# Batch 0 of an FNet and gated-FFN kernel: even sequence rows regrouped by s mod 4 and summed as two 64-row tiles over half the columns

## The chip, the cores and the metric

The kernel runs on one core of one Trainium2 chip. The metric is the device time of one execution in microseconds (us). The engines are named as the profile names them: PE is TensorE (matmul; PEld is its weight load), DVE is VectorE, ACT is ScalarE, POOL is GpSimd, SP is SyncE, which issues nearly all transfers; SPq is its queue.

## What is computed

```python
batch, seq, dim = 8, 3008, 256                  # x: float32
X = np.fft.fft(x, axis=1); X = np.fft.fft(X, axis=2)
t = X.real.astype(np.float32).reshape(24064, 256)
gate = 1.0 / (1.0 + np.exp(-(t @ w_gate)))      # w_gate, w_val: 256 x 1536
out  = (gate * (t @ w_val)) @ w_out             # w_out: 1536 x 256
```

The three weights come as float64 and are brought to float32 on the chip, piece by piece.

## The kernel before

**Sequence transform.** With S = 3008 and M = S/2, the four rows s, S-s, M+s and M-s are folded into each other, so that a batch has 768 row slots (s from 0 to 752, the rest weighted zero). They lie as s = 6p + q: partition p of 128, slot q of 6. `half_rows` does this fold for batch 0 on DVE, in four steps over the slots `(0, 1)`, `(2, 3)`, `(4,)`, `(5,)` (`SLICES`). The folded rows are matmul weights (128 rows by 128 features); what streams past them are the tables `ST[0]` (cosine) and `ST[1]` (sine), each with 128 partitions, 6 slots and 753 columns: 377 even frequencies (`NE`), then 376 odd ones (`NO`). Because s = 6p + q, the parity of q is the parity of s. `half` keeps the sums over even slots in one PSUM bank (`ev`) and those over odd slots in another (`od`); `places` writes ev + od to frequency k and ev - od to M - k, for the cosine into the tile `pk`, for the sine into `qk`. `e_sums(1)` does the same for the one feature column that stands by itself: weights of one column, cosine table only, four column groups of PE (`at_`), result `er`, stored to DRAM as `ed`.

Later batches come in another way (`quarter`: four tiles of 32 rows); the change does not touch them.

**Weights.** `weight_load(j)` loads piece j (512 KB), `weight_parts(j)` takes its two halves apart on ACT, `weight_join(j)` puts them together with three DVE instructions and one POOL addition, and `weight_use(j)` calls `merge`, which multiplies the piece with the feature transform `dt` on PE and copies the two results out on ACT to `G2` and `G1`.

**Main loop.** Step i handles 128 of the 1536 hidden units for 252 frequencies: `front_a` (weights G1, streams `pk`) and `front_b` (weights G2, streams `qk`) fill the bank `pf`, `gate_a` and `gate_b` make the gated product, `back` multiplies with w_out. In the first steps the loop also merges the later weight pieces: piece 2 right after `front_b(0)`, pieces 3 and 5 around `front_b(1)`, and so on.

**Order.** The order of each engine is the order of the program text. The part before the loop is written out by hand: first all loads on SP, in the order in which they are to be used, then weight pieces 0 and 1, then four steps of fold and sums, then `places`. Every transfer from SP takes one of eight completion semaphores in turn, and waits for the transfer that had it before.

**Transfers of other shapes.** Two kinds of transfer later in this kernel matter for reading the change. `run` (L163) copies rows of the next batches from DRAM to DRAM with access patterns of 4 by 32 by 256 elements on both sides. `table_rows` (L206) copies rows of the tables to `rtab`, in DRAM too, with patterns of 2 by 32 by 753 on both sides. The loads at the start have 128 partitions as the outermost size of the side in SBUF, and 128 or 512 rows in DRAM.

```python
    def load_rows(q, n):
        nc.sync.dma_start(out=X[0][0:NP, :, q : q + n], in_=xf[0, :, :, q : q + n])
    def load_table(t, q, n, lo=0, hi=NE + NO):
        nc.sync.dma_start(out=ST[t][0:NP, q : q + n, lo:hi], in_=stab[:, t, q : q + n, lo:hi])
```

Of the kernel before, what the change touches and what calls it, by code (L numbers as in the profile page):

```python
# [8 lines left out]
F32 = mybir.dt.float32  # L9
# [3 lines left out]
ALU = mybir.AluOpType  # L13
# [68 lines left out]
def kernel(  # L82
# [52 lines left out]
    def bank(name, other=None):  # L135
        if other is not None:
            return pso.tile([P, 512], F32, name=name, tag=f"po{other}")
        return psx.tile([P, 512], F32, name=name, tag="x")
# [49 lines left out]
    table = const.tile([2, 1], F32, name="table")  # L188
    ed = dram.tile([B, NK + 1], F32, name="ed")

    def load_rows(q, n):
        nc.sync.dma_start(out=X[0][0:NP, :, q : q + n], in_=xf[0, :, :, q : q + n])  # L192

    def load_table(t, q, n, lo=0, hi=NE + NO):
        nc.sync.dma_start(out=ST[t][0:NP, q : q + n, lo:hi], in_=stab[:, t, q : q + n, lo:hi])

    NQ4 = NE // 4 + 1
    TILES = [(g, par, par * HP + g * TB) for g in range(2) for par in range(2)]
# [204 lines left out]
    def weight_use(j):  # L403
        w, c = jobs[j]
        if w == 2:
            WO[c] = WS.pop(j)
        else:
            merge(WS.pop(j), w, c, (4, 2, 3)[next(turns) % 3] if j > 1 else None)

    def merge(ws, g, c, other):  # L410
        cs = slice(c * WC, (c + 1) * WC)
        ps = bank("ps", other)
        for h in range(2):
            for t in range(2):
                mm(ps[:, h * WC : (h + 1) * WC], dt[:, t, h * HD : (h + 1) * HD], ws[:, t, :],
                   h == 0 and t == 0, t == 1)
        nc.scalar.copy(G2[:, g, cs], ps[:, WC : 2 * WC])
        nc.scalar.copy(G1[:, g, cs], ps[:, 0:WC])
        for f in range(c * WC // P, (c + 1) * WC // P):
            nc.sync.dma_start(  # L420
                out=ge[:, g, f : f + 1], in_=G2[0:1, g, f * P : (f + 1) * P])
# [60 lines left out]
    TURN = {}  # L482
    MORE = {}

    SLICES = ((0, 1), (2, 3), (4,), (5,))

    def fold_ops(b, nq):
        x4 = X.pop(b)
# [40 lines left out]
        if b:  # L529
            ops += [lambda q=q: feat(pool, *parts[1], q) for q in qs]  # L530
            for i, op in enumerate((ALU.add, ALU.subtract)):
                for ds in (slice(0, HD), slice(HD, D)):
                    ops.append(lambda i=i, op=op, ds=ds: pool.tensor_tensor(
                        x4[:, 3, i * N3 : (i + 1) * N3, ds], x4[:, 1, 0:N3, ds],
                        x4[:, 1, N3:, ds], op=op))
            parts[0] = x4[:, 3], x4[:, 1]
            slots = x4.rearrange("p i q d -> p (i q) d")
            tan = TAB["tan"], TAB["less"]

            def swap(blk):  # L540

                hs, here, there = (((1, 3), slice(0, HD), slice(HD, D)), ((0, 2), slice(HD, D), slice(0, HD)))[blk]
                for g, par, lo in TILES:
                    o = lo + (TB, -TB)[g]
                    for h in hs:
                        nc.sync.dma_start(out=x4[lo : lo + TB, h, :, there], in_=x4[o : o + TB, h, :, here])

            def more(v, blk, c, q):

                here, there = ((slice(0, HD), slice(HD, D)), (slice(HD, D), slice(0, HD)))[blk]  # L550
                here, there = (v[..., ds] for ds in (here, there))
                nc.vector.scalar_tensor_tensor(out=here, in0=there, scalar=c[:, q : q + 1], in1=here,
                                               op0=ALU.mult, op1=ALU.add)
            MORE[b] = ([lambda: swap(0), lambda: swap(1)],
                       [lambda q=q, a=a: more(slots[:, 9 + q : 19 + q : 9] if a == 0 else slots[:, (0, 21, 6)[a] + q],
                                              0, TAB[("other", "cx", "cy")[a]], q)
                        for q in range(N3) for a in range(3)],
                       [lambda q=q, a=a: more(slots[:, q + N3 : q + N3 + 10 : 9] if a else slots[:, q : q + 16 : 15],
                                              1, TAB["other"][:, N3:], q) for q in range(N3) for a in range(2)])

            def turn(q, minus):

                y = [slots[:, q : q + 16 : 15], slots[:, q + N3 : q + N3 + 10 : 9]]
                if minus:
                    y.reverse()
                nc.vector.scalar_tensor_tensor(
                    out=y[0][:, :, HD:D], in0=y[1][:, :, 0:HD], scalar=tan[minus][:, q : q + 1],
                    in1=y[0][:, :, 0:HD], op0=ALU.mult, op1=ALU.add)
            TURN[b] = [lambda q=q, minus=minus: turn(q, minus) for q in range(N3) for minus in range(2)]
            ops += [lambda q=q: feat(pool, *parts[0], q) for q in qs]  # L570
        else:

            def half_rows(q):
                even, odd = slice(0, 4, 2), slice(1, 4, 2)
                point(nc.vector, even, odd, q)
                first(nc.vector, even, odd, q)
                for blk in range(2):
                    across(nc.vector, blk, q)
                v, r = x4[:, 0:2, q], x4[:, 2:4, q]
                for to, op in ((r, ALU.subtract), (v, ALU.add)):  # L580
                    nc.vector.tensor_tensor(to[:, :, :, 1:HD], v[:, :, :, 1:HD], v[:, :, :, D - 1 : HD : -1],
                                            op=op)
                nc.vector.memset(r[:, :, :, 0:1], 0.0)
            ops += [lambda q=q: half_rows(slice(q[0], q[-1] + 1)) for q in SLICES]
        for blk, (v, r) in enumerate(parts):
            if b and blk:
                W[b, blk] = v[:, :, HD:D], r[:, :, HD:D]
# [4 lines left out]

    PQE = {}

    def half(b, w, d, blk, sn, other=None):


        c0, n = ((0, NE), (NE, NO))[blk]
        ev, od = [bank(name, other and other[i])[:, 0:n] for i, name in enumerate(("ev", "od"))]

        def sums(*qs):
            for q in sorted(qs, key=lambda q: q % 2):
                mm((ev, od)[q % 2], w(q), ST[int(sn)][0:NP, q, c0 : c0 + n], q < 2, q >= NQ - 2)

        def then():
            a = evp.tile([P, NE], F32, name="a", tag="a")[:, 0:n]
            nc.scalar.copy(a, ev)
            return lambda: places(d, blk, sn, a, od)
        return sums, then

    def places(d, blk, sn, ev, od, ends=(0, 1)):
        if 0 in ends:
# [64 lines left out]
        for t in PQE[b]:  # L677
            nc.vector.memset(t[:, NK:], 0.0)

    def seq_group(b, blk, what, other=None):  # L680
        return half(b, lambda q: W[b, blk][what][:, q, :], PQE[b][what], blk, what == 1, other)


    def e_load(b):
        nc.sync.dma_start(out=x8[:, b - 1], in_=xf[b, :, :, :, HD : HD + 1])

# [9 lines left out]
    def e_sums(m=B - 1):  # L696


        ps = bank("pe", NB - 1)
        at_ = lambda blk, par: slice((2 * blk + par) * TB, (2 * blk + par) * TB + m)  # L700

        def sums(*qs):
# [249 lines left out]
    nc.gpsimd.dma_start(out=zero, in_=nil)  # L952
    nc.scalar.dma_start(out=dt, in_=dtab.rearrange("(c p) d -> p c d", p=P))
    load_x(0)
    for j in range(2):
        weight_load(j)
    load_rows(0, 2)
    load_table(0, 0, 2)
    load_rows(2, 2)
    load_table(1, 0, 2, 0, NE)  # L960
    load_table(0, 2, 2)
    load_rows(4, 1)
    load_table(0, 4, 1)
    load_rows(5, 1)
    weight_load(2)
    load_table(1, 2, 2, 0, NE)
    load_table(0, 5, 1)
    load_table(1, 4, 2, 0, NE)
    load_table(1, 0, NQ, NE)
    for j in (3, 5, 6, 8, 9, 4, 7):  # L970
        weight_load(j)

    e0 = shared["qk"][:, 4 * WC : 4 * WC + CH]
    nc.gpsimd.memset(e0, 0.0)
    weight_parts(0)
    weight_parts(1)
    weight_join(0)
    weight_join(1)
    warm = bank("warm", 2)
    for i in range(4):  # L980
        mm(warm[:, 0:WC], dt[:, 0, 0:P], dt[:, 0], True, True)
    weight_use(0)
    weight_use(1)
    seq_start(0)

    cos = [seq_group(0, blk, 0, (2 * blk, 2 * blk + 1)) for blk in range(2)]
    e_, e_even = e_sums(1)
    sin = [seq_group(0, 0, 1)]
    for q, f in zip(SLICES, fold_ops(0, 2), strict=True):
        f()  # L990
        e_(*{1: (0, 1), 5: (2, 3, 4, 5)}.get(q[-1], ()))
        sin[0][0](*{5: (3,)}.get(q[-1], ()))
        cos[0][0](*q)
        cos[1][0](*q)
        sin[0][0](*{1: (0, 1), 4: (2,), 5: (4, 5)}.get(q[-1], ()))
    places_c = [cos[blk][1]() for blk in range(2)]
    weight_parts(2)
    weight_join(2)
    rest, *ends = e_even()
    rest()  # L1000
    for f in ends:
        f()
    for f in places_c:
        f()
    nc.scalar.copy(e0[0:1], E0[0][:, 0:CH])
    weight_parts(3)
    weight_join(3)
    sin.append(seq_group(0, 1, 1, (0, 1)))
    sin[1][0](*range(NQ))
    for j in range(KEEP, KEEP + 3):  # L1010
        weight_load(j)
    places_s = [group[1]() for group in sin]
    for f in places_s:
        f()
    e_rows(0)

    per = NFT * len(chunks)
# [2 lines left out]
    def at(i, *fs):  # L1020
        side.setdefault(i, []).extend(fs)
# [21 lines left out]
    for i, f in zip((1, 2, 2, 2, 3, 4, 4, 4, 5, 6, 6, 8, 8, 8, 9, 9, 9, 9, 10, 10, 10, 11, 11), quarter_x(1), strict=True):  # L1043
        at(i, f)
    at(i0 + 1, lambda: load_x(1))
    for b in range(1, B):
        at(20 + b, lambda b=b: e_load(b))
    at(3 * i0, e_fold)
# [197 lines left out]
```

## Time and profile before

| | |
|---|---|
| median of 3 runs | 1908.45 us (1908.44 to 1908.66) |
| profiled execution, its time | 1909.15 us |
| its span in the profile | 1907.4 us |
| PE busy | 1895.6 us (99%) |
| POOL, DVE, ACT busy | 1543.4, 1520.6, 1353.2 us |
| first `pf` matmul of the main loop | at 33.05 us |
| granted TensorE clock | 1.00 |

The span runs from the first to the last instruction of the program; 1.75 us of the execution lie around it. From the first `pf` matmul on, PE works through the rest of the program with almost no gap, so the stretch before it is looked at by itself: it holds the loads, the fold, and the sums of batch 0. A "pass" below is one matmul row of the profile; each float32 matmul of the program makes two.

### The profile page before, as it was taken

The numbers are of one execution on the slowest core, as the hardware profiler recorded it, in microseconds if no ns is written. First come the engines' busy times: TensorE is split into PE (matmuls) and PEld (weight loads), VectorE is DVE, ScalarE is ACT, GpSimd is POOL, SyncE is SP. The second block draws the span as 40 slices with busy tenths as digits, with TensorE's granted clock in tenths as the row PEclk, the third lists the DMA queues.
The fourth block names the chain that finished last, engine by engine and source line by source line (L and its number), as shares of the span: only waits on it lengthen the run. The fifth ranks groups of instructions, "written<-read, shape, count | busy, mean of one in ns | idle before, by whom it ended". The sixth has DMA issues, their size and how long they took to land.

```text
span 1907.4 us, 36057 instructions
## 1 busy us (share of the span) xinstructions
PE 1895.6 (99%) x11836; PEld 1756.6 (92%) x11836; DVE 1520.6 (80%) x3375; ACT 1353.2 (71%) x3235; POOL 1543.4 (81%) x2733
## 2 busy tenths in 40 slices
PE   8999999999999999999999999999999999999999
PEld 5788999999999999999999999999999999999998
DVE  7678888878979778897788878888788777977775
ACT  4777777777777777777777777677767777777775
POOL 2489879987999779997799878999789986877770
PEclk9999999999999999999999999999999999999999
DMA  8446221212022121211211212122120110010001
GB/s 315 120 134 80 71 89 51 72 33 81 21 64 54 31 87 32 62 41 37 89 39 48 45 39 81 40 52 58 30 74 17 36 37 15 15 25 17 15 18 30
DMA packets 197333, 109.33 MB, mean 57 GB/s; under 512 B 134823, under 2 KB 188818, under 8 KB 195354
## 3 DMA queue, kind: packets, MB, share of 16 engines
q1 hardware_dynamic: 196568, 106.50, 21.1%
q8 instruction: 95, 1.56, 0.3%
q14 instruction: 92, 0.75, 0.1%
q10 hardware_dynamic: 546, 0.51, 0.1%
q0 software_dynamic: 32, 0.00, 0.0%
HBM read 71.24 MB, written 47.87 MB: 62 GB/s over the span
## 4 chain that ended last, share of the span: by engine, by line
PE 94%; DMA 2%; SPq 1%; POOL 1%; ACT 1%; DVE 0%; issue 0%; ACTq 0%; POOLq 0%
PE pf L133 49%; PE po L133 41%; PE sum L133 2%; DMA rtab<-in_stab_dram 1%; PE ps L133 1%; POOL sf L824 1%; DMA st<-in_stab_dram 1%; SPq L206 1%; DMA raw<-in_moe_w_val_dram 0%; PE od L133 0%; POOL x L507 0%; SPq L192 0%; SPq L375 0%; PE pe L133 0%; PE ev L133 0%
## 5 line engine op out<-in xcount | busy, mean ns | idle before, releaser
L824 POOL TENSOR_TENSOR sf<-h,sf 128x168 f32<-128x168 f32 (+1 forms) x1104 | 621.0, 582 | 79.5 <-DVE h L818 75.9
L824 POOL TENSOR_TENSOR sf<-h 128x168 f32<-128x168 f32 (+1 forms) x920 | 519.3, 584 | 159.8 <-DVE h L818 158.0
L133 PE MATMUL pf<-qk,G 128*128 128x252 f32 (+1 forms) x2304 | 583.4, 376 | 0.9 <-ACT ae L787 0.8
L133 PE MATMUL pf<-pk,G 128*128 128x252 f32 (+1 forms) x2304 | 582.7, 376 | 0.0
L772 ACT ACTIVATE pf<-ek,ge 128x252 f32<-128x252 f32 (+1 forms) x1142 | 538.2, 471 | 23.2 <-DMA ge<-G 3.0
L133 PE MATMUL po<-sf,wf 128*128 128x168 f32 (+1 forms) x2944 | 508.3, 305 | 0.0
L787 ACT ACTIVATE ae<-pf 128x504 f32<-128x504 f32 (+1 forms) x576 | 338.8, 588 | 218.7 <-PE pf L133 217.2
L133 PEld LDWEIGHTS pf<-pk,G 128*128 128x128 f32 x2304 | 435.9, 190 | 53.3 <-ACT pf L772 1.5
L133 PE MATMUL po<-h,wf 128*128 128x168 f32 (+2 forms) x2584 | 461.3, 307 | 0.0
L133 PEld LDWEIGHTS po<-sf,wf 128*128 128x128 f32 x2944 | 453.4, 190 | 8.0
L818 DVE TENSOR_TENSOR h<-pf,z 128x252 f32<-128x252 f32 (+1 forms) x576 | 240.4, 417 | 274.0 <-ACT pf L815 270.5
L802 DVE TENSOR_TENSOR z<-ae,pf 128x504 f32<-128x504 f32 (+1 forms) x576 | 384.6, 668 | 83.1 <-ACT h L801 79.1
L908 DVE TENSOR_TENSOR c<-c 128x168 f32<-128x168 f32 (+1 forms) x920 | 438.7, 500 | 3.3
L133 PEld LDWEIGHTS pf<-qk,G 128*128 128x128 f32 x2304 | 410.6, 190 | 32.3 <-ACT ae L787 2.1
L133 PEld LDWEIGHTS po<-h,wf 128*128 128x128 f32 x2584 | 410.4, 190 | 17.8 <-issue 0.9
L801 ACT ACTIVATE h<-pf 128x252 f32<-128x252 f32 (+1 forms) x576 | 216.9, 376 | 146.3 <-PE pf L133 129.0
L815 ACT ACTIVATE pf<-z 128x252 f32<-128x252 f32 (+1 forms) x576 | 214.3, 372 | 116.4 <-DVE h L814 114.5
L814 DVE TENSOR_TENSOR h<-h,pf 128x252 f32<-128x252 f32 (+1 forms) x576 | 232.9, 404 | 0.0
L824 POOL TENSOR_TENSOR sf<-sf 128x168 f32<-128x168 f32 (+1 forms) x184 | 101.7, 553 | 14.4
L824 POOL TENSOR_TENSOR sf<-sf,h 128x168 f32<-128x168 f32 (+1 forms) x184 | 110.1, 598 | 0.0
L891 ACT COPY c<-po 128x504 f32<-128x504 f32 (+1 forms) x138 | 78.5, 569 | 0.0
L918 DVE STREAM_TRANSPOSE os<-c 128x256 f32<-128x256 f32 x188 | 76.5, 427 | 0.1
(158 smaller groups left out, 876.4 us busy)
## 6 DMA issues: line engine op xcount, KB each, us to landing
x<-xr SPq DMA_DIRECT2D x14, 1536.0 KB
out_dram<-os SPq DMA_DIRECT2D x376, 56.0 KB
xr<-in_xf_dram SPq DMA_DIRECT2D x105, 128.0 KB
x<-x SPq DMA_DIRECT2D x112, 96.0 KB
xr<-in_xf_dram SPq DMA_DIRECT2D x14, 384.0 KB
ek<-ed SPq DMA_DIRECT2D x40, 126.0 KB
out_dram<-os SPq DMA_DIRECT2D x288, 7.0 KB
xr<-in_xf_dram SPq DMA_DIRECT2D x21, 124.0 KB
```

What stands on the lines that cost most here:

```text
L133: nc.tensor.matmul(o, l, r, start=start, stop=stop, skip_group_check=True)
L772: nc.scalar.activation(PF[i][:, g], EK[i // NFT], AF.Copy, scale=ge[:, g, f : f + 1])
L787: nc.scalar.activation(AP[i], PF[i], AF.Copy, scale=2.0)
L801: nc.scalar.activation(H[p][:, fh, 0:n], PF[i][:, 0], AF.Sigmoid)
L802: nc.vector.tensor_tensor(z[:, :, ::-1], AP.pop(i), PF[i], op=ALU.subtract)
L814: nc.vector.tensor_tensor(h[:, fh, 0:n], h[:, fh, 0:n], pf[:, 1], op=ALU.mult)
L815: nc.scalar.activation(pf[:, 0], z[:, 0], AF.Sigmoid)
L818: nc.vector.tensor_tensor(h[:, fh, n:], pf[:, 0], z[:, 1], op=ALU.mult)
L824: nc.gpsimd.tensor_tensor(block(p, dst), block(p, a), block(p, b), op=(ALU.subtract, ALU.add)[op])
L891: (nc.vector.tensor_copy if t == 1 or t == 3 else nc.scalar.copy)(C[0][:, 3 * t * R : 3 * (t + 1) * R], PO[t][:, 0 : 3 * R])
L908: nc.vector.tensor_tensor(t[:, dst * R : (dst + 1) * R], *v, op=(ALU.subtract, ALU.add)[op])
L918: nc.vector.transpose(os_[0][0][:, s, 0:nb, h, :], t[:, c0 : c0 + nb * TB])
```

## The change

Slots 0, 2 and 4 (even s) are filled anew. `PAIR` names, for each of the three, one residue of s modulo 12 that goes to partitions 0 to 63 (s divisible by 4) and one that goes to partitions 64 to 127 (s = 2 modulo 4). `pair` makes the access pattern in DRAM: it takes two rows out of every pair of old partitions and puts the choice between the two outermost (size 2), then 64, then the row. `load_rows` uses it for an even slot, in four transfers (one for each of the four folded rows); `load_table` uses it for an even slot of a table.

`seq_sums` takes the place of `half`. For even slots it sums the two halves of the partitions separately (`x` and `y`, two banks), each as a 64-row tile, and only over the columns `H0` to `H1`, 377 of 753; `join` makes the other columns from sums and differences of x and y. Odd slots are as before: 128 rows, all columns. The order before the loop is new: the odd slots 1 and 3 are loaded, folded and summed first; weight piece 1 is loaded, joined and merged late; the outer columns of the cosine table's even slots, which only `e_sums` reads, come as six more transfers. `load_again` restores the cosine table's even slots to the old order in step 20 of the loop, for a later use. In `e_sums(1)` the order of slots becomes 1, 3, then 0, 2, 4, 5.

```diff
+    PAIR = {0: ((0, 0), (0, 2)), 2: ((0, 4), (1, 0)), 4: ((1, 2), (1, 4))}
+    def pair(ap, q, i):
+        n = ap.shape[1]
+        lo, hi = ((n * two + i) * NQ + r for two, r in PAIR[q])
+        flat = ap.rearrange("(m two) i q k -> m (two i q) k", two=2)
+        return flat[:, lo : hi + 1 : hi - lo].rearrange("m t k -> t m k")
+    def load_rows(*qs):
+        for q in qs:
+            if q % 2:
+                nc.sync.dma_start(out=X[0][0:NP, :, q], in_=xf[0, :, :, q])
+            else:
+                for h in range(4):
+                    nc.sync.dma_start(out=X[0][0:NP, h, q], in_=pair(xf[0], q, h))
+    H0, H1 = NE // 2, NE + NO // 2
+    def load_table(t, q, lo=0, hi=NE + NO):
+        src = stab[:, t, q, lo:hi] if q % 2 else pair(stab, q, t)[:, :, lo:hi]
+        nc.sync.dma_start(out=ST[t][0:NP, q, lo:hi], in_=src)
+    def load_again():
+        for q in range(0, NQ, 2):
+            nc.sync.dma_start(out=ST[0][0:NP, q], in_=stab[:, 0, q])
...
-    SLICES = ((0, 1), (2, 3), (4,), (5,))
+    SLICES = (slice(1, 4, 2), slice(0, 3, 2), slice(4, 5), slice(5, 6))
...
+        def even(*qs):
+            for q in qs:
+                for blk, (lo, n, to) in enumerate(cols):
+                    for h in range(2):
+                        rows = slice(h * HP, (h + 1) * HP)
+                        mm((x, y)[h][:, to : to + n], w[blk][rows, q], ST[what][rows, q, lo : lo + n],
+                           q == blk == 0, q == NQ - 2)
...
-    for j in range(2):
-        weight_load(j)
-    load_rows(0, 2)
-    load_table(0, 0, 2)
...
-    load_table(1, 0, NQ, NE)
-    for j in (3, 5, 6, 8, 9, 4, 7):
+    weight_load(0)
+    load_rows(1, 3)
+    for q in (1, 3):
+        load_table(0, q)
+    load_rows(0, 2)
+    for q in (1, 3):
+        load_table(1, q)
+    load_rows(4)
+    for q in (0, 2, 4):
+        load_table(0, q, H0, H1)
+    load_rows(5)
+    for q in (0, 2, 4):
+        load_table(1, q, H0, H1)
+    weight_load(1)
+    for t in range(2):
+        load_table(t, 5)
+    for q in (0, 2, 4):
+        load_table(0, q, 0, H0)
+        load_table(0, q, H1)
+    for j in (2, 3, 5, 6, 8, 9, 4, 7):
         weight_load(j)
...
+    next(folds)()
+    odd(0, 1, 3)
+    odd(1, 1, 3)
+    odd_s(0, 1, 3)
+    e_(1, 3)
+    next(folds)()
+    even(0, 2)
+    next(folds)()
+    even(4)
+    a = copy()
+    next(folds)()
+    pk = join(a)
+    HELD[1] = bank("ps")
+    od_s.append(bank("od"))
+    odd_s(1, 1, 3)
+    even_s(0, 2, 4)
+    odd(0, 5)
+    odd(1, 5)
+    weight_parts(1)
+    a = copy_s()
+    weight_join(1)
+    for blk in range(2):
+        pk(blk, 0)
+    qk = join_s(a)
+    odd_s(0, 5)
+    e_(0, 2, 4, 5)
+    qk(0, 0)
+    rest, last, end = e_even()
+    rest()
+    weight_use(1)
+    odd_s(1, 5)
+    last()
+    nc.vector.tensor_copy(e0[0:1], E0[0][:, 0:CH])
+    weight_parts(2)
+    qk(1, 0)
+    weight_join(2)
...
+    at(20, load_again)
```

## The prediction

> **What bounds the kernel now.** I read the page first: PE is busy 1895.6 of 1907.4 us, so a change that leaves the main loop alone pays only by moving the loop's start. Second, the chain of waits in order of time, for the first 60 us (start, length, what):
>
> ```profile
> 14.43 9.31 DMA st<-in_stab_dram
> ...
> 23.78 0.90 PE ev L133 x2
> 24.68 1.37 PE pe L133 x16
> 26.05 2.10 PE od L133 x6
> ...
> 33.21 4.25 PE pf L133 x20
> 37.46 3.45 PE ps L133 x16
> 40.91 0.90 PE pf L133 x4
> 41.81 1.73 PE ps L133 x8
> ```
>
> Up to 23.7 us the chain is loads; then PE works off the sums, and from `pf` on it never stops. The last line is the merge of weight piece 5; "before" reaches it at 41.81 us, and I measure the shift there, because after it every step has room.
>
> So transfers matter, and the third view is the stages: length; PE, PEld, DVE, ACT, POOL busy (and instructions); clock, DMA share, GB/s.
>
> ```profile
> 3.00:24.00 21.00, 16.30 (x57) 10.12 (x58) 17.12 (x34) 4.50 (x10) 3.44 (x2) 1.00 1.05 383
> 85.00:96.00 11.00, 11.00 (x39) 7.30 (x38) 7.87 (x18) 8.39 (x24) 6.75 (x14) 1.00 0.28 98
> 110.00:120.00 10.00, 10.00 (x59) 9.39 (x58) 7.96 (x20) 7.57 (x21) 9.39 (x18) 1.00 0.14 52
> ```
>
> The first row is the loads at the start: all 16 DMA engines full, 383 GB/s, 24 GB/s each. The other two are stretches in which only one kind of copy runs, with more copies waiting. The SP queue's timeline names them (start, length, what), and the SP queue's line among the DMA queues for 110 to 120 us gives its share (packets, MB, share of 16 engines):
>
> ```profile
> 83.03 8.81 SPq L163 DMA_DIRECT2D xr<-in_xf_dram  x6
> 100.43 17.66 SPq L206 DMA_DIRECT2D rtab<-in_stab_dram  x6
> q1 hardware_dynamic: 170, 0.50, 12.9%
> ```
>
> L163 copies patterns of 4 x 32 x 256: 98 GB/s, four engines' worth. L206 copies 2 x 32 x 753: 12.9% of 16 is two engines, 0.50 MB in 10 us is 50 GB/s. SP stands still on them meanwhile: six issues last 17.66 us. A copy's outermost size thus sets how many engines carry it, and copies that follow one another use the same engines, since eight may be in flight and still the rate stays that of one.
>
> **The change part by part.**
>
> *Paired loads.* `pair` gives the DRAM side the sizes 2 x 64 x n; the SBUF side has 128 partitions. There are 12 such copies of rows (128 KB, 1.573 MB), 6 half tables (128 x 377 columns, 1.158 MB) and 6 outer cosine pieces (128 x 188 columns, 0.578 MB): 24 copies, 3.309 MB. No row of "before" has 2 on one side and 128 on the other, so two prices bound it: two engines (L206: 49 GB/s, with the 24.5 GB/s per engine of both rows), 3.309 MB / 49 = 67.5 us; sixteen engines (383 GB/s), 8.6 us. I take two engines: L206 is the nearest row, since it reads the same tensor with the same outermost 2, and whoever deals out rows must walk both sides in step.
>
> The Trainium skill, "DMA: Bandwidth & Descriptors", section "Why a DMA increments its semaphore by 16 and not by 1", states that a copy goes to the largest number of engines up to 16 that divides the slowest size (1 left out) of both sides, and to the lowest-numbered ones. By that rule 128 against 2 gives two engines, the same two for all 24 copies, and the sum is the one below. L163 and L206 agree with it (98 and about 50 GB/s); they can't show the mixed case.
>
> *When the last load lands.* The other bytes in front of the last outer piece: weight 0 and 1 and `dt` 1.31 MB, odd rows 1.573, odd table slots 2.313, together 5.2 MB at 383 GB/s = 13.6 us. They can't overtake: a full copy needs a share on each engine, behind the paired copies there. Start and landing: in "before" 7.68 MB were asked for up to the table piece whose wait ends at 23.74; 7.68 / 383 is 20.05, so 3.7 us. Sum: 3.7 + 13.6 + 67.5 = 84.8 us. What could be cheaper is bounded by 421 GB/s, the best rate of the trace (102 to 108 us), 26.3 per engine: 62.9 + 12.3 + 3.7 = 78.9. Dearer: the slowest full slice during the row loads, 354 GB/s, 22.1 per engine: 74.8 + 14.7 + 3.7 = 93.2.
>
> *Who waits.* PE is in order. The last wait stands before the column sums over slot 4 (outer columns); behind it are the merge of piece 1, the last sine sums and the whole main loop. SP waits too, each copy for the one eight before it; behind stand weights 2 to 7, one share of 1.4 us each (512 KB / 383), needed later than that.
>
> *From there to the merge of piece 5*, by durations of "before": last column sums 0.75; ACT copies `z` twice, with its wait 1.1; DVE two `er` instructions 1.0; ACT `ae` 0.47; DVE third `er` 0.54 and the copy to `e0` 0.4 (ACT's row; DVE has none); `qk` 0.46; join of piece 2, 1.55; `qk` 0.46; join of piece 3, 1.5; four `places`, 1.85; join of piece 5, 1.5; POOL's addition 1.3; semaphores 0.2: 13.1 us. PE in that time has 0.75 + 1.73 + 0.63 + 3.4 + 0.85 + 3.45 + 0.85 = 11.7 us of work, so DVE's decoding is late, not PE. But PE will have idled: the first eight warm passes took 3.3 us where eight later ones of the same shape take 1.73. If that slowness returns, PE has 13.3: no more than 0.4 us on top.
>
> *What lies under the loads and costs nothing while they are late.* Even sums: before 24 passes of 0.316 us (7.6 us); now 48 passes of half the columns in pairs. Row tiles overlap here: the later batches' `sum` tiles make 96 passes of 95 columns in 2.93 us, 0.122 for four where one alone streams 0.080. So a pair costs 0.158 to 0.20: 3.8 to 4.8 us, a gain of 2.8 to 3.8 (none if the two tiles run in turn). Column sums: slots of one parity keep two column groups busy instead of four, 1.27 + 1.9 us instead of 0.7 + 1.37: 1.1 more. About three more switches between full and tiled matmuls, 0.2 each by the gaps around `pe`: 0.6. The folds are the same instructions with another stride: 0. `join`: four more DVE instructions, 1.9 us. Piece 1 later: DVE 1.6 and POOL 1.3 us earlier free, given back later. If that cover is gone, see the first rival. Twenty-one more issues on SP, 0.34 to 0.6 us each as in "before": under the copies' own 2.7 us. `load_again`: three ordinary copies, 1.16 MB, 3 us of DMA around 115 us, read first by the later column sums at 181 us: 0.
>
> *Sum.* 84.8 + 13.1 = 97.9, less 41.8: 56.1 us. The profiled execution was 1909.15 us (span 1907.4 and 1.75 around it), 0.7 above the median of the runs shown; on the median the sum is 1964.5.
>
> **The rivals.**
>
> *1. The paired copies spread over all sixteen engines (not slower).* For it: the side in SBUF has 128 partitions, as in every load of the first stage row. Against it: L206. Then the rows of slots 0 and 2 are there at 3.65 MB / 383 + 3.7 = 13.3 us; fold 4.1, fold of slot 4 2.55, its sums 0.8, ACT's copy 0.65, sine sums 1.4, 2.0 and 2.1, column sums 2.0 end at 28.9; from there 12.4 us (13.1 less the first 0.75) give 41.3, against 41.8: 1908. PE's own work saved, 2.4 us at most, is the floor: 1906. If the two row tiles ran in turn, even sums cost 2.5 more on that path: 1911. All within 0.2%, which is 3.8 us and about what a measurement of this kernel can tell from no change. It decides if a paired copy moves above some 350 GB/s; at 100 the loads already cost 24 us more.
>
> *2. Copies of two engines each, but on pairs that rotate.* Eight in flight would fill all engines: 24 copies in three rounds, a round as long as its longest copy (193 KB / 49 = 3.9 us) and up to the 3.7 us of start and landing, 11.7 to 22.8 us where sixteen engines take 8.6: 1911 to 1922. Against it: six L163 copies in a row stay at 98 GB/s.
>
> *3. One engine only.* 3.309 MB / 24.5 = 135 us, 67.5 more: 2032. Nothing in the trace shows a copy with a size of 2 on one engine.
>
> **How the numbers follow.** Forecast 0.85; rival 1, 0.10; rival 2, 0.02; rival 3, 0.03. Slower by over 0.2%: forecast, rival 3 and half of rival 2, 0.89. Within: the rest of rivals 1 and 2, 0.10. Faster: 0.01, since the floor of rival 1 misses 0.2%. The range is that of the forecast: low 78.9 + 13.1 - 41.8 = 50.2, 1958.6; high 93.2 + 13.5 - 41.8 = 64.9, 1973.4; one us more on each side for the reading of the landing.
>
> **What the changed profile would show.** Right: the stage from 15 to 80 us near 50 GB/s and a DMA share of 0.13; SP issues of even rows lasting 2.7 us; PE mostly idle until the column sums near 85 us; first `pf` near 89; a slow first merge; the merge of piece 5 near 98; the main loop no different. Wrong: 380 GB/s in that stage and first `pf` near 32 us (rival 1); 24 GB/s (rival 3); paired copies whose landings overlap (rival 2). Even sums of about 0.16 to 0.20 us a pair would bear out the tiles, though they can't pay here.

## The result, and the profile after

The changed kernel takes 1977.13 us (median of 6 runs, 1976.06 to 1978.25) against 1908.45 us before (6 runs, 1908.29 to 1909.24): 1.0359 times as long, 95% interval 1.0346 to 1.0372. The profiled execution is 1976.86 us, its span 1975.1, so 67.7 us more span than before. The mean granted clock is 0.984, where before it was 1.00.

The chain of waits of the changed kernel (start, length, what):

```profile
15.81 2.70 SPq L206
...
18.56 2.70 SPq L206
...
80.11 9.09 DMA st<-in_stab_dram
...
89.24 1.43 PE pe L133 x6
90.67 3.71 PE ps L133 x8
94.38 0.78 PE od L133 x2
95.19 0.55 DVE qk L656
...
109.16 1.54 PE pf L133 x6
110.70 1.73 PE ps L133 x8
```

Before, the loads left the chain at 23.78 us; now SP's queue and the paired copies hold it to 89.24. L206 issues the rows of an even slot (128 KB, one every 2.74 us), L212 the tables. Behind the last wait stands what the prediction put there: column sums, merge of piece 1 (`ps`, 3.71 us instead of 1.73), the last sine sums, and then DVE. The merge of piece 6, the last line, is at 45.24 us before: 65.5 us of the 67.7 are lost by here.

The stages (length; PE, PEld, DVE, ACT, POOL busy; clock, DMA share, GB/s):

```profile
30.00:40.00 10.00, 5.45 (x12) 1.49 (x12) 4.07 (x7) 0.00 (x0) 0.00 (x0) 0.50 0.14 49
70.00:80.00 10.00, 6.93 (x16) 3.09 (x17) 4.20 (x9) 1.59 (x3) 1.29 (x1) 0.50 0.14 48
```

That is where 383 GB/s stood before: 48 GB/s at a seventh of the sixteen engines, two engines' worth. In both stretches PE waits for loads between its sums, and its clock is granted at half. PE's waits (us in total, times, longest) name the rest:

```profile
PE u L133 <- DMA st<-in_stab_dram: 19.3, 4, 10.7
PE od L133 <- DMA st<-in_stab_dram: 17.2, 1, 17.2
...
PE pf L133 <- ACT pf L811: 2.0, 1, 2.0
PE pf L133 <- ACT G L440: 1.7, 1, 1.7
```

The last two are losses that the prediction did not have. The one of 1.7 us (ending at 109.16) is PE waiting for ScalarE's copy of piece 5's merge; the one of 2.0 us ends at 231.55, deep in the main loop, and its chain is this:

```profile
225.35 5.08 DMA ek<-ed
230.51 0.48 ACT pf L811
231.02 0.48 ACT pf L811
231.55 1.12 PE pf L133 x4
```

The load `ek` was issued at 157.69 us before. With the shift of 65.46 us it was due at 223.15; it went out at 225.35, because `load_again`'s three issues stand ahead of it on SP.

### The profile page after: what moved, and what is told of

Its sections match the earlier page's. It is cut to its first block, busy times and chain, and to the rows that moved or that the text cites. A ratio compares the mean times of both kernels' runs of the same rounds, so it can differ in the third digit from the quotient of the medians.

```text
span 1975.1 us, 36139 instructions
## 1 busy us (share of the span) xinstructions
PE 1914.6 (97%) x11860; PEld 1765.4 (89%) x11860; DVE 1525.1 (77%) x3380; ACT 1351.0 (68%) x3232; POOL 1543.3 (78%) x2733
## 4 chain that ended last, share of the span: by engine, by line
PE 91%; SPq 4%; DVE 2%; POOL 1%; ACT 1%; DMA 1%; issue 0%; ACTq 0%; POOLq 0%
PE pf L133 48%; PE po L133 40%; PE sum L133 2%; SPq L212 2%; SPq L206 1%; POOL sf L863 1%; PE ps L133 1%; DMA st<-in_stab_dram 0%; DVE c L947 0%; DVE z L841 0%; SPq L203 0%; DMA ek<-ed 0%; POOL x L529 0%; SPq L396 0%; ACT pf L811 0%
```

## The experiments

The theory: the two outermost sizes (2 in DRAM, 128 in SBUF) put every paired copy on two engines, and that is nearly all of the loss; the rest are four small losses behind it. The rivals: the copies are slow for another reason (small pieces, their number), or the new order of sums is slow by itself. The first four runs are one execution each; the six of the changed kernel spread over 2.2 us, so there the traces count for more than the times.

**Rows to 64 partitions.** The same number of copies, the same bytes, the same pieces of 1 KB, but 64 is outermost on both sides. Tables are left as they are.

```diff
-                for h in range(4):
-                    nc.sync.dma_start(out=X[0][0:NP, h, q], in_=pair(xf[0], q, h))
+                for g in range(2):
+                    for h in range(0, 4, 2):
+                        nc.sync.dma_start(out=X[0][g * HP : (g + 1) * HP, h : h + 2, q],
+                                          in_=half_of(xf[0], q, g)[:, h : h + 2])
...
+    def half_of(ap, q, g):
+        two, r = PAIR[q][g]
+        return ap.rearrange("(m two) i q k -> two m i q k", two=2)[two, :, :, r]
```

> The changed kernel, but the twelve copies of even rows take 64 partitions and two of the four folded rows each instead of 128 partitions and one: as many copies, as many bytes, the same 1 KB pieces, outermost size 64 on both sides instead of 2 against 128. Tables stay paired. Theory (the outermost size of 2 puts a copy on two engines): the rows take 12 x 0.38 us on sixteen engines instead of 12 x 2.74 us, the last load lands 28 us earlier (near 61 us), the time is 1949 us. Rival (small copies of 1 KB pieces, eight in flight, are slow as such): no change, 1977 us.

Measured: 1950.57 us beside 1908.87 for the kernel before on the same chip. The chain has the last wait here:

```profile
62.52 1.43 PE pe L133 x6
63.95 3.60 PE ps L133 x8
```

89.24 has become 62.52 us: 26.7 us, where twelve such copies at 2.74 us had taken 32.9. Bytes, pieces and the number of copies are the same; what differs is that 64 stands outermost on both sides and that each copy reaches 64 partitions. The rival that the pieces or their number are slow falls.

**Outer cosine pieces to 64 partitions**, two copies for each of the six that come last.

```diff
+        if q % 2 == 0 and lo != H0:
+            for g in range(2):
+                nc.sync.dma_start(out=ST[t][g * HP : (g + 1) * HP, q, lo:hi], in_=half_of(stab, q, g)[:, t, lo:hi])
+            return
         src = stab[:, t, q, lo:hi] if q % 2 else pair(stab, q, t)[:, :, lo:hi]
```

> The changed kernel, but each of the six outer cosine pieces is loaded as two copies of 64 partitions. Theory: they leave the two engines (6 x 2.3 us there) and land by about 76 us; PE's own chain at half clock from the last half table (72.4 us) then sets the end of the column sums near 82 us instead of 90.6: 1968 us, or 1965 if the loads still set it. Rival (number of small copies counts): twelve copies instead of six, 1977 us or more.

Measured: 1970.39 us, somewhat less gained than expected.

```profile
79.21 3.65 PE pe L133 x15
82.86 1.93 PE ps L133 x8
```

The half tables, still on two engines, now set the column sums. Gone are 6.7 us, about half of the 13.8 us that the six issues lasted; PE's sums, 3.65 us in one piece, had been hidden between the landings. And the merge of piece 1 takes 1.93 us: PE had worked without a gap since 75.11 us (4.1 us of odd sums, then the column sums), and its clock had come up at 81.0.

**Repeated loads later.** `at(20, load_again)` becomes `at(26, load_again)`.

> The changed kernel with the three restoring copies of the cosine table moved from step 20 to step 26 of the loop, behind the load of ek for the next chunk. Theory (they hold up the ek load in SP's queue by 2.2 us, and PE waits 2.05 us for it at 231 us): that wait is gone, 1975.0 us. Rival (the wait comes from the load on the DMA engines or from the shift itself): it stays, 1977 us.

Measured: 1974.06 us, and no wait of PE at 231 us is left. So that stall was SP's queue, as read above. Not all of the 3.1 us gained is the stall: from the last wait (89.53) to the merge of piece 5 (104.49) this run takes 14.96 us instead of 15.85, because the merge of piece 1 takes 2.90 instead of 3.71. Nothing in the edit touches that stretch; the clock came up earlier in it (92.76 us instead of 94.53).

**PE kept busy.** Seven matmuls into a bank that nobody reads stand between the column sums.

```diff
-    e_(0, 2, 4, 5)
+    e_(0)
+    keep(3)
+    e_(2)
+    keep(4)
+    e_(4, 5)
```

> The changed kernel with seven matmuls of no use put between the column sums of slots 0, 2 and 4, so that PE does not idle before the last load lands. Theory (after idling PE runs at half its clock for some 4 us, which makes the merge of piece 1 take 3.7 us instead of 1.73, and DVE's qk waits for the sine sums behind it): from the last landing to the merge of piece 5 it takes 13.5 to 14 us instead of 15.85, 1975 us. Rival (DVE's own chain is what is long): 15.85 stays, 1977 us.

Measured: 1975.36 us. From the last wait (89.56) to the merge of piece 5 (103.59) it is 14.03 us where the changed kernel took 15.85. The clock is granted in full from 79.4 us on, and the merge of piece 1 takes 1.99 us. So 1.8 of the 2.75 us that the prediction missed in this stretch were PE at half clock in the profiled execution; the run before shows that some 0.9 of them come and go between executions. Against the profiled execution of the changed kernel this run gained 1.5 us in all; the stall at 231 us was still there, 2.4 us long.

**All paired copies to 64 partitions**, with `load_again` at step 20 and at step 26: the two edits above, the rows as one copy for each half of a slot, the tables without the condition on `lo`.

> The changed kernel with all its paired copies (rows, half tables, outer pieces) made as two copies of 64 partitions each, so that no copy has an outermost size of 2. Theory (only the two engines made it slow): the last load lands near 26 us, the time is the first rival's, 1908 to 1911 us; with the ek load still held up by the restoring copies, 2 us of it are that. Rival (the new order, the late piece 1 or the tiles are slow by themselves): 1915 us or more.

> The same with the restoring copies in step 26 instead of step 20. Theory: 2 us less than the kernel with all copies of 64 partitions, 1906 to 1909 us, so at or just under the kernel before. Rival: as slow as that one, if the wait for ek was caused by something else.

Measured: 1923.61 us, ratio 1.0079 (1.0065 to 1.0093), and 1920.78 us, ratio 1.0058 (1.0044 to 1.0072). Four fifths of the loss are gone, but both miss by 12 us: the number of the rival, though its reason (the new order) is only part of it, as the plain copies below show. The stages, first of the kernel before and then of the one with step 26:

```profile
10.00:25.00 15.00, 13.09 (x55) 6.88 (x57) 14.26 (x32) 3.05 (x8) 2.15 (x1) 1.00 1.05 379
```

```profile
10.00:25.00 15.00, 10.87 (x52) 5.94 (x52) 10.03 (x23) 1.12 (x3) 0.00 (x0) 1.00 1.08 254
25.00:35.00 10.00, 7.88 (x42) 3.79 (x42) 6.88 (x18) 1.58 (x3) 1.29 (x1) 1.00 0.64 193
```

All sixteen engines are busy (1.08), yet they move 254 GB/s. A piece of 1 KB took 78 ns in the median, 47 ns before, and 46 ns in the runs with plain copies below. After 25 us the share falls to 0.64: SP, at 0.6 us an issue, can't ask for 48 KB fast enough. The last load lands at 36.8 us; the kernel before ended its last wait for a load at 23.74. My theory that 16 engines mean full rate falls. The Trainium skill, "SBUF — State Buffer", section "Door 1: The DMA port swizzle (why `[64,N]` ≈ `[32,N]`)", has a rule that the expectation left out: 64 partitions reach only half of SBUF's ports. It gives about 218 GB/s for such a copy; 218 GB/s from 10 to 15 us and 254 in the whole stretch, which mixes them with full copies, agree.

**Plain copies of the same sizes.** So that the price of the order is seen by itself, each paired copy becomes a plain one. The even slots then hold rows in the old order, so these runs leave out the regrouping, and their sums are not the transform; instructions and bytes are those of the change.

```diff
-                    nc.sync.dma_start(out=X[0][0:NP, h, q], in_=pair(xf[0], q, h))
+                    nc.sync.dma_start(out=X[0][0:NP, h, q], in_=xf[0, :, h, q])
...
-        src = stab[:, t, q, lo:hi] if q % 2 else pair(stab, q, t)[:, :, lo:hi]
+        src = stab[:, t, q, lo:hi]
```

> The changed kernel with each paired copy replaced by a plain one of the same size, pieces and place in the queue: 128 partitions, one source row each. The even slots then hold rows that are not the paired ones, so this part of the computation is wrong; instructions, their order and the bytes loaded stay those of the changed kernel. It gives the worth of the regrouping if its loads cost what loads cost before. Theory A (all that is left of the loss is in the loads): the last piece lands near 26 us as the table of before did, the 14.1 us from the last landing to the merge of piece 5 bring that merge to 40 us against 41.8 before, 1.66 us are lost at the wait for ScalarE's copy and about 2 us at 231 us behind the repeated loads: 1909 to 1911 us. Theory B (the order of sums and joins is slow by itself): merge of piece 5 later than 43 us, 1913 us or more.

> The same with the repeated cosine loads at step 26 instead of 20 (the even slots again hold unpaired rows). Theory A: the stall at 231 us goes, 1907 to 1909 us, 2 us under the run with step 20. Theory B: 1911 us or more.

Measured: 1916.87 us, ratio 1.0039 (1.0027 to 1.0052), and 1912.88 us, ratio 1.0022 (1.0013 to 1.0032). Theory B's numbers. 60.3 of the changed kernel's 68.7 us hung on the paired loads (1977.13 less 1916.87), 4.0 lie between step 20 and step 26, and 4.2 remain, with no wait of PE for a load of rows or tables left (DVE's folds still wait 2.4 us for rows, which they do not in the kernel before). From 10 to 25 us the plain copies move 328 and 359 GB/s with the same small pieces; 64 partitions had moved 254, and against the second run they cost some 8 us (1920.78 less 1912.88).

The 4.0 us are not the stall alone. In the profiled execution with step 20 PE waits 2.5 us for ScalarE behind the late `ek` (0.3 with step 26), and then its clock is granted at half for 3.4 us, which costs another 1.7:

```profile
171.00:174.50 3.50, 3.50 (x14) 3.35 (x13) 3.50 (x9) 1.73 (x4) 3.50 (x6) 0.51 0.32 11
```

By their mean clock the five executions have this or not: two at 1.000 took 1914.15 and 1914.79 us, three at 0.999 took 1916.87 to 1918.12.

The chain of the second run shows where the 4.2 us are:

```profile
27.75 2.06 PE pe L133 x12
...
30.80 0.54 DVE er L649
...
35.64 1.26 DVE wqk L406
...
47.05 1.54 PE pf L133 x6
48.59 1.73 PE ps L133 x8
```

The column sums come last among PE's sums but for two passes. Before, they ran from 24.68 to 26.05 us and the sine sums stood behind them, so DVE's first `er` began at 27.15 us. Now it begins at 30.80, 3.65 us later, and the merge of piece 6 comes at 48.59 instead of 45.24, 3.35 us later. PE did gain what the prediction said: the sine part's even sums take 2.12 us for 12 pairs, 0.177 each. But behind the column sums DVE is now the longer chain, and a gain on PE ahead of it is worth nothing. From the first `er` to DVE's first gate step `z` PE is the busy engine before (first line), and DVE here (second line; its longest pause is 0.5 us):

```profile
27.15:40.19 13.04, 13.04 (x54) 9.83 (x53) 11.02 (x22) 7.95 (x17) 3.33 (x3) 1.00 1.00 350
```

```profile
30.80:43.85 13.05, 11.71 (x50) 8.94 (x50) 12.21 (x23) 8.66 (x18) 3.93 (x3) 1.00 0.78 264
```

This is read from the traces. The two runs that follow were to show it by experiment and do not: each put another wait in DVE's way.

**Column sums ahead of the sine part's even sums**, plain copies as above.

```diff
-    even_s(0, 2, 4)
     odd(0, 5)
     odd(1, 5)
+    e_(0, 2, 4, 5)
+    rest, last, end = e_even()
+    rest()
+    even_s(0, 2, 4)
     weight_parts(1)
...
     odd_s(0, 5)
-    e_(0, 2, 4, 5)
     qk(0, 0)
-    rest, last, end = e_even()
-    rest()
...
```

> The run with plain copies and late repeated loads (1912.9 us; its even slots hold unpaired rows), with the column sums of slots 0, 2, 4, 5 moved ahead of the even sums of the sine part, their edge row's joins with them, and the outer cosine pieces loaded ahead of the sine halves. In the run without this move VectorE's first join of the edge row starts at 30.80 us against 27.15 before, and the merge of piece 6 at 48.59 against 45.24: the same 3.4 us. Theory A (the chain behind the column sums sets the end of the opening, and the new order starts it late): the join starts at 27 to 28 us, the merge of piece 6 falls to 45 to 46 us, 1908 to 1910 us. Theory B (the two wider joins and the decoding of piece 1, which stand in the same stretch of VectorE, set it): the merge stays at 48 us or later, 1912 us or more.

Measured: 1917.47 us, ratio 1.0043 (1.0031 to 1.0056): a miss, and worse than without the move. `er` does begin at 27.96 us as expected, but:

```profile
33.14 2.01 PE ps L133 x8
...
35.42 1.00 DVE qk L649 x2
...
51.45 1.73 PE ps L133 x8
```

The first line is the merge of piece 1. Its decoding now stands behind the edge row's copies on ScalarE, and PE waits 3.3 us for it. What counts is DVE: in the run without the move it decoded piece 1 from 24.25 us on, ahead of `er`; here it stands idle then, 3.71 us up to `er`, 1.09 before the decoding and 0.51 before `qk`. That is 5.3 us of idle time from there to `qk` instead of 2.6, about the 2.9 us by which the merge of piece 6 is later. Moving one step of an in-order queue forward moved the wait to another.

**Pieces 0 to 2 as the kernel before has them**, with the early column sums: 0 and 1 loaded and decoded first, 2 loaded in the middle.

> The run with plain copies and the early column sums (1917.5 us; its even slots hold unpaired rows), with the weight pieces as the kernel before has them: 0 and 1 loaded and decoded first, 2 in the middle of the loads and decoded before the joins of the edge row; the cosine joins stand ahead of the edge row's, and the merge of piece 1 behind the last sine sums. In the run without this PE waited 3.28 us at 33.1 for the decoded piece 1, and VectorE was busy without a break from 31.6 us to the merge of piece 5. Theory A (VectorE's work behind the column sums is the bound of the new order, and the late piece 1 is what lengthens it): the first join of the edge row at 27 to 28.5 us, the chain behind it shorter by the 1.5 us of one decode, the merge of piece 6 at 45.2 to 46.5, 1908 to 1910 us. Theory B (the joins through a scratch tile, 4 operations of 0.55 us, and what waits for them lengthen it by themselves): the merge at 47 us or later, 1911 us or more.

Measured: 1914.96 us, ratio 1.0034 (1.0021 to 1.0046). A miss too, although it lies below the run without it. PE's waits and the chain:

```profile
PE od L133 <- DVE x L598: 2.9, 1, 2.9
```

```profile
30.63 0.54 DVE er L649
...
50.67 1.73 PE ps L133 x8
```

DVE decodes piece 1 ahead of the odd fold now, and one small instruction of the fold lasts 1.25 us instead of 0.16, beside an addition of POOL. The fold ends at 15.0 us instead of 12.8, PE's first sums wait 2.9 us for it, and in the profiled execution they then run in part at half clock (5.68 us instead of 4.07). The column sums are no earlier than with the late piece 1. `weight_join(2)` was still behind `qk`, so the decode that the expectation takes off the chain had stayed on it: this run does not test that term.

**64 partitions with fewer copies and early sums**, and **64 partitions from two queues** (the even cosine tables whole in both; in the second the upper half of each pair is issued by ScalarE, and the order of sums is that of the change).

```diff
     for q in (0, 2, 4):
-        load_table(0, q, H0, H1)
+        load_table(0, q)
...
-                nc.sync.dma_start(out=ST[t][g * HP : (g + 1) * HP, q, lo:hi], in_=half_of(stab, q, g)[:, t, lo:hi])
+                (nc.sync, nc.scalar)[g].dma_start(out=ST[t][g * HP : (g + 1) * HP, q, lo:hi],
+                                                  in_=half_of(stab, q, g)[:, t, lo:hi])
```

> The run with every paired copy as two copies to 64 partitions and late repeated loads (1920.8 us), with the same move of the column sums, and with the cosine tables of the even slots loaded whole: 6 copies in place of 18. The paired loads took 1.0 to 1.1 of the queues' time at 218 to 276 GB/s and then, at 30 to 35 us, the issues of small copies bound at 77 GB/s. Theory A (issues and small pieces held the last landing at 36.8 us): the cosine tables land by 29 to 31 us, the join of the edge row starts at 31 to 33 us, 1912 to 1915 us, slower than before still. Theory B (the rate of copies to 64 partitions bounds whatever their size): the last landing stays beyond 33 us, 1917 us or more.

> Every paired copy as two copies to 64 partitions with late repeated loads (1920.8 us when all were issued on SP), the order of sums unchanged, the even cosine tables whole (6 copies in place of 18), and the copy to the upper 64 partitions of each pair issued from ScalarE's queue, so that copies to both halves are under way together and SP issues half as many. With all on SP the stretch from 10 to 25 us moved 218 to 276 GB/s at a full queue share. Theory A (copies to one half of the partitions at a time are what is slow): 330 GB/s or more in that stretch, last landing at 26 to 30 us, 1913 to 1916 us. Theory B (each piece of such a copy is slow whatever runs beside it): 220 to 280 GB/s again, last landing at 32 us or later, 1917 us or more. ScalarE's nine issues of about 0.6 us stand ahead of its first decoding step in both.

Measured: 1925.68 us, ratio 1.0093 (1.0077 to 1.0108), and 1927.51 us, ratio 1.0098 (1.0084 to 1.0112). Both slower than the plainer version. Their stages:

```profile
10.00:25.00 15.00, 10.64 (x46) 5.70 (x45) 9.31 (x19) 0.65 (x2) 0.00 (x0) 0.95 1.09 254
```

```profile
10.00:25.00 15.00, 0.40 (x1) 0.40 (x2) 4.25 (x8) 1.21 (x2) 2.14 (x1) 0.59 1.08 263
```

254 and 263 GB/s at a full share: neither pieces of 3 KB nor two queues change the rate. A piece of 3,012 bytes took 184 to 189 ns in the median, 127 ns before. That agrees with the Trainium skill, "SBUF — State Buffer", section "Can I just issue two DMAs to hit both halves?", which says that two copies to the two halves serialize. The times of the two runs themselves say little about the rate. In the first the column sums start at 31.45 us and wait for no load, where 64 partitions with small pieces had waited until 36.97: fewer copies did end the landing earlier, as theory A had it, and the time is long because of the wait of 3.3 us for piece 1 again. In the second ScalarE was held up among its own issues:

```profile
5.49 14.42 ACTq L218 DMA_DIRECT2D st<-in_stab_dram  x6
19.96 0.66 ACT L413 ACTIVATE raw<-raw 128x512 f32<-128x512 f32 x1 [17.73 <-DMA st<-in_stab_dram]
```

The six issues last 0.47 to 0.61 us each, but they stretch over 14.42 us: ScalarE waits between them, and the trace puts the wait down to copies of the tables that had not landed. The decoding of piece 0 began at 19.96 us, and PE waited 15.3 us for it. The "nine issues of about 0.6 us" had the length of an issue right and left out the waits between them.

No version run is faster than the kernel before.

## Why the prediction was right and wrong

The forecast was 1964.5 us, between 1958.6 and 1973.4; measured are 1977.13. The mechanism that carried the forecast held. PE's last wait for a load ends at 89.24 us, inside the 78.9 to 93.2 that the prediction gave. The step that failed is the one behind it: the sum from the landing to the end was 7.0 us too low, and the range had let only 0.4 us of it vary.

- **Two engines for a paired copy: right.** A row copy of 128 KB every 2.744 us is 47.8 GB/s. The rule of the Trainium skill that the prediction cites ("DMA: Bandwidth & Descriptors", section "Why a DMA increments its semaphore by 16 and not by 1") had given two engines for 128 against 2, and the trace agrees (a DMA share of 0.14 of sixteen). That the outermost sizes decide is shown by two runs together: rows of the same pieces with 64 on both sides gained 26.7 us, and plain copies of the same sizes to 128 partitions ran at a share of 1.01 to 1.05.
- **The term of 67.5 us for 24 copies: too small by 3.8.** The 49 GB/s came from rows of 3 KB (753 floats). The trace has 12 row copies of 1 KB pieces in 32.9 us, six half tables at some 4.1 us (47 GB/s) and six outer pieces of 752 bytes at 2.3 us (42 GB/s): 71.3 us. One rate was taken for three sizes. The last wait ends at 89.24 instead of 84.8, 4.4 us later; the other 0.6 us lie in the full copies or in start and landing, and were not told apart.
- **From the landing to the merge of piece 5: 15.85 us instead of 13.1.** The list of steps was right, two of their prices were not. The prediction let a slow PE cost 0.4 us, on the ground that PE had 11.7 us of work against DVE's 13.1. But the slow merge of piece 1 lies ahead of the last sine sums, and DVE's `qk` waits for those: slowness of PE goes straight into DVE's chain. Kept busy, PE gave 1.8 us back; how much of it an execution pays varies (0.9 us less in the run with late repeated loads). The other 0.9 us is one decoding step of piece 3, 1.26 us instead of 0.35, which stands beside an addition of POOL; that cause was read from the trace and not tested.
- **"After it every step has room": wrong, 2.2 us.** 1.65 us of it are PE's wait, behind the merge of piece 5, for ScalarE's copy of that merge. Every run with the new order has this wait; the kernel before has not.
- **`load_again` priced at 0: wrong, 2.05 us in the trace.** The prediction asked who reads the loaded data, and not who is queued behind the three issues on SP, though it asked just that of the first loads. The pairs of runs give 2.8 and 4.0 us by their medians for step 20 against step 26; the larger one holds the stretch at half clock as well.
- **These four terms** add up: 4.4 + 2.75 + 2.2 + 2.05 = 11.4 us, and 56.1 + 11.4 = 67.5 of the 67.7 us.
- **Even sums, column sums, switches at no cost under the loads: right here.** 0.177 us a pair at full clock lies in the 0.158 to 0.20 given. With fast loads they would still not pay in this order, as the plain copies show.
- **Rival 1, sixteen engines at 1906 to 1911 us.** The plain copies come near that case (328 GB/s in the profiled execution, where the prediction asked for some 350): 1916.87 us. Its sum put the end of the column sums at 28.9 us, and the trace has 29.8. Missing from it were the 0.9 us of the decoding step, the wait for ScalarE's copy and `load_again` with the half clock behind it, the same terms as above. So with its loads at the rate of plain copies the change would still have been slower by over 0.2%, and the chances given to "within" stood on a sum that was too low.

What stays open: whether DVE's chain alone makes the 4.2 us of the plain copies, or DVE's 2.4 us of waiting for rows has a part in them, which no run told apart; and whether some order of these sums and decodings comes level with the kernel before. Three were run with plain copies, 4 to 8.5 us slower; none was better on all its queues at once.

## What to carry to other kernels

A regrouping by access pattern has to be priced at the copy first: look at the outermost sizes of both sides, and then at how many partitions one copy reaches, since either can cost more than the arithmetic saves. When a step is moved, list for every in-order queue that it enters what stands behind it; here that was three of the four losses that the prediction missed (`qk`, ScalarE's copy, `ek`), and it spoilt the last four experiments. And before a gain on one engine is counted, ask which engine's chain is the longer one behind it: PE's shorter even sums lay ahead of a chain that DVE set.

## What the runs showed of the hardware

- Stretches of copies to 64 partitions keep all sixteen engines busy and still move only 254 to 263 GB/s, with pieces of 1 or 3 KB and from one queue or two. Plain copies to 128 partitions move 328 to 359 with the same small pieces, and the larger ones of the kernel before 379.
- The granted clock fell to 0.50 while PE waited for loads, and with it a `ps` pass went from 0.216 to 0.427 us. Between two changes the clock stays as it is for whole multiples of 3.413 us in every trace here. In the changed kernel it rose at 94.53 us, 5.3 us after the last wait, so the merge of piece 1 ran at the low clock throughout (3.71 us); in the run with late repeated loads it rose 3.2 us after the last wait, and the same merge took 2.90 behind the same 1.43 us of column sums. The Trainium skill, "TensorE: Matmul & The Clock Gate", section "Part 1: The HAM clock gate (the "warmup" mystery)", gives a window of about 3.4 us in both directions, and the multiples agree with it.
- Issues on ScalarE's queue can hold that engine's arithmetic: six of them, 0.47 to 0.61 us each, stretched over 14.42 us with waits between them, and the ACTIVATE behind them started at 19.96 us.
